# Blocks two and three of a Mamba-2 scan with an ELU layer behind it: twelve of sixteen groups through the word products instead of eight

## The chip, the cores and the metric

One Trainium2 chip, one of its cores. The metric is the device time of one execution in microseconds (us). The kernel before was run three times: 350.15 us in the median, 349.95 to 351.11. One further execution was profiled.

A core has engines that run beside each other, each taking its own instructions strictly in the order in which they were written: TensorE (PE in the profile, PEld for its weight loads), VectorE (DVE), ScalarE (ACT), GpSimd (POOL) and SyncE (SP, which issues most of the transfers). They meet only where one waits for another's semaphore.

## What is computed

A chunked state-space scan over four batches, eight heads and 768 tokens, and behind it a dense layer of width 2048 with ELU, all in float32 accuracy:

```python
cum = np.cumsum(log(a), axis=-1)                    # within a chunk
L   = np.exp(cum[..., :, None] - cum[..., None, :]) * causal
y   = ((C @ B^T) * L) @ x  +  (C @ state) * exp(cum)
state = exp(sum(log a)) * state + (B * exp(cum[-1] - cum))^T @ x

h = y @ w_in                      # [3072, 256] @ [256, 2048]
g = where(h > 0, h, exp(min(h, 0)) - 1)
out = g @ w_out                   # [3072, 2048] @ [2048, 256]
```

The weights arrive as 64-bit numbers and are turned into float32 on the chip.

## The kernel before, in words

**Blocks and groups.** The tokens are twelve blocks of 256, numbered 0 to 11; blocks go in pairs. The hidden width 2048 is sixteen groups `m` of 128, and eight pieces `i` of 256 (two groups each). `w_in` and `w_out` come as eight pieces each. Piece 0 to 7 is `w_in`, piece 8 + j is the part of `w_out` that `l2(n, j)` multiplies.

**Two ways for the first layer.** `l1(n, i)` (matmuls at L667) multiplies one block by one piece of `w_in` in plain float32: four products of 128x256, each of which is two passes in the trace, so eight records. Its ELU is `elu()`: a Relu and an Exp on ACT (L680, L687) and one subtraction with maximum on DVE (L689). `l1_words(n, m)` (L787) multiplies a pair of blocks (512 tokens) by one group, with numbers that were split into words: three passes, high word by high word and low by low into one PSUM tile `high`, the sum of words by the sum of words into another, `both`, two records each. Its end is longer: ACT scales `both` into e (L793), DVE combines it with `high` (L796), ACT takes Relu and Exp (L802, L803, in `begin_end`), DVE takes the maximum (L810, in `end_words`). **The order matters:** inside `l1_words` the L793 of this group is written first, then the L810 of the group before, then the L796 of this group; `begin_end` follows. For even groups `end_words` also subtracts one half of g from the other on POOL (L845).

**Words.** `words_of_w(i)` makes the high word of a piece of `w_in` on ACT (L736) and the sum of words on DVE (L737); `low_of_w(i)` the low word with two subtractions on POOL (L845). `words_of_y(n)` makes y1 on ACT (L755, L757; partly on DVE, L759) and y0 on DVE (L762); `both_of_y(n)` y_both with two operations on DVE (L772). y1 and y0 have one buffer each, so the words of the next pair can only be written when the last `l1_words` of this pair has read them.

**Second layer.** Blocks 0 and 1 go through `l2(n, j)` (L829). From block 2 on pairs go through `second(n)`, a seven-product scheme on sums and differences of quarters of g and of `w_out` (L904), whose quarters `quarters(n, i)` picks from g; those of pieces that went through `l1` lie otherwise than those that went through `l1_words`, and need a subtraction on DVE (`sum_t1`, L858).

**Making a piece of a weight.** `w_take(i, eng)` takes the absolute value on ACT (L196), the low part on the named engine (DVE at L209 or ACT at L205) and the sign on DVE (L223); `w_give(i)` clips (L231) and joins with the sign (L238) on DVE and adds the low part on POOL (L248, `w_sum`).

**The scan.** `spread_cum(n)` loads the running sums of a block, spread over the partitions, into a tile L (two buffers). `decay_of(n, h)` turns one head of it into exp(L - cum) with two small ACT instructions (L521, 128x64 each, the subtraction as the bias `ncum`), and after every fourth head two POOL instructions mask it (L526). `scores(n)` (L541), `sums(n)` (L571), `weigh(n, q)` (DVE, L550), `states(n)` (DVE L588 and POOL L593, which makes Sx), `across(n)` (L616) and `inside(n)` (L634, then copies into yT on ACT, L651) do the rest.

**PSUM.** Seven tiles of one bank are shared by everything but the sums of the second layer. An `l1` holds one until its L689 has run, an `l1_words` two until its L810; `scores` takes four.

**The order around the change** is written out by hand. A first loop, `for s, (n, i)`, has twelve `l1`: in its steps 0 to 7 it runs `decay_of(2, s)`, in step 7 `scores(2)` and `sums(2)`, in step 9 half of the decays of block 3, and in every odd step up to 11 one piece. A second loop, `for j in range(2 * DIRECT)`, runs `l2(0, j)` and one `l1` in each of eight steps (block 2 in the first four, block 3 in the others), pieces 11 to 15 of the weights in steps 0, 2, 3, 4 and 5, the scan of block 3, the decays of blocks 4 and 5 and the words of y. A third loop, `for j in range(8, 16)`, runs `l1_words(2, 8)` to `l1_words(2, 15)`, `l2(1, ...)` and the scan of blocks 4 and 5. Then a loop over pairs from block 4 on has sixteen `l1_words` each, with the products of `second` in between.

Of the kernel before, what the change touches and what calls it, by code (L numbers as in the profile page):

```python
# [20 lines left out]
CW = 256  # L21
WORD = 2.0 ** 12
NEAR = 1.0 + 2.0 ** -13
DIRECT = 4


def high_word_as_f32(word):
# [5 lines left out]
def kernel(  # L33
# [118 lines left out]
                w_load(piece)  # L152


    w_order = [(i + DIRECT) % (DF // CW) for i in range(DF // CW)]
    w_in = [None] * (DF // CW)
    for i in w_order:
        w_in[i] = conv.tile([P, KC, CW], F32, tag="w_in", name="w_in", bufs=DF // CW + 1)
# [306 lines left out]
    def turn_part(n, part):  # L465
        if part < 2:
            turn_square(n, 1 - part)
        elif part == 2:
            mask_heads(n)
        else:  # L470
            turn_exp(n)
# [41 lines left out]
    def decay(n, q):  # L513

        decay_of(n, 2 * q)
        decay_of(n, 2 * q + 1)

    def decay_of(n, h):
        L, row = st[n]["L"], rows_of(n).start + NG * h
        for u in range(2):  # L520
            nc.scalar.activation(  # L521
                L[:, h, u], L[:, h, u], ACT.Exp, bias=ncum[:, u, row:row + 1])
        if h % 4 == 3:
            for v in range(2):
                part = L[Q * v:Q * v + Q, h - 3:h + 1]
                nc.gpsimd.affine_select(  # L526
                    out=part, in_=part, pattern=[[0, 4], [0, 2], [1, Q]],
                    compare_op=ALU.is_ge, fill=0.0, base=0, channel_multiplier=-1)

# [218 lines left out]
    def words_of_y(n):  # L750

        y = yT[n // 2].rearrange("p k b u i -> p k (b u i)")
        y1 = conv.tile([P, KC, 2 * BLK], F32R, tag="y1", name="y1", bufs=1)
        y0 = conv.tile([P, KC, 2 * BLK], F32R, tag="y0", name="y0", bufs=1)
        nc.scalar.activation(y1[:, 1], y[:, 1], ACT.Copy, scale=NEAR / WORD)  # L755
        if n == 4:
            nc.scalar.activation(y1[:, 0], y[:, 0], ACT.Copy, scale=NEAR / WORD)  # L757
        else:
            nc.vector.tensor_scalar(  # L759
                out=y1[:, 0], in0=y[:, 0], scalar1=NEAR / WORD, scalar2=None, op0=ALU.mult)  # L760
        for k in range(KC):
            nc.vector.scalar_tensor_tensor(  # L762
                out=y0[:, k], in0=y1[:, k].bitcast(F32), scalar=WORD, in1=y[:, k],
                op0=ALU.mult, op1=ALU.subtract)
        y_words[n] = y1, y0
# [11 lines left out]
    def l1_words(n, m, between=None):  # L777

        cols = slice(m % 2 * P, (m % 2 + 1) * P)
        w, w0 = k_words[m // 2]  # L780
        w1, both_w, w0 = w[:, 0, :, cols], w[:, 1, :, cols], w0[:, :, cols]
        y1, y0, both_y = y_words[n]
        high, both = psum([P, 2 * BLK], "ps_h"), psum([P, 2 * BLK], "ps_w")
        passes = [(high, w1, y1), (high, w0, y0), (both, both_w, both_y)]
        for ps, lhs, rhs in passes if n > 2 and m == 0 else passes[2:] + passes[:2]:
            for k in range(KC):
                nc.tensor.matmul(  # L787
                    out=ps, lhsT=lhs[:, k], rhs=rhs[:, k], start=k == 0 and lhs is not w0,
                    stop=k == KC - 1 and lhs is not w1)
        if between:  # L790
            words_of_y(between)
        e = ffn.tile([P, 2 * BLK], F32, tag="e", name="e", bufs=2)
        nc.scalar.activation(e, both, ACT.Copy, scale=WORD)  # L793
        if late:
            end_words()
        nc.vector.scalar_tensor_tensor(  # L796
            out=high, in0=high, scalar=WORD - 1.0, in1=e, op0=ALU.mult, op1=ALU.add)
        late.append((n, m, high, e))
# [8 lines left out]
    def end_words():  # L807
        n, m, h, e = late.pop(0)
        g_of[n, m] = ffn.tile([P, 2, BLK], F32, tag=f"g{m % 2}", name="g", bufs=12)
        nc.vector.scalar_tensor_tensor(  # L810
            out=g_of[n, m].rearrange("p b i -> p (b i)"), in0=e, scalar=1.0, in1=h,
            op0=ALU.subtract, op1=ALU.max)
        if m % 2 == 0 and (n, m) != (2, 14):
            sub(g_of[n, m][:, 1], g_of[n, m][:, 1], g_of[n, m][:, 0])

    def row_of(n):
# [39 lines left out]
    def sum_t1(n, i, eng=nc.gpsimd):  # L856
        b11, b21, b12, b22 = quarters(n, i)
        eng.tensor_tensor(out=b12, in0=b12, in1=b11, op=ALU.subtract)  # L858
# [107 lines left out]
    def w_take(i, low):  # L966

        w_abs(i)
        w_low(i, low)
        w_sign(i)  # L970
# [117 lines left out]
    w_load(10)  # L1088
    write_flat(2)

    todo = 5
    for s, (n, i) in enumerate((
            (1, 0), (1, 1), (1, 2), (0, 4), (1, 3), (0, 5), (1, 4), (0, 6), (1, 5), (0, 7),
            (1, 6), (1, 7))):
        l1(n, i, parts=2 if s < 2 else 1)
        if s < 8:
            decay_of(2, s)
        if s == 7:
            st[0] = kept
            scores(2)  # L1100
            sums(2, 0, pool=p_o, tag="o", parts=(None, last))
            weigh(2, 0)
            weigh(2, 1)
        if s % 2 == 1 and todo < 11:
            w_take(todo, nc.vector)
            w_give(todo)
            w_load(todo + 6)
            todo += 1
        if s in (1, 3):
            load_bc(3, us=(s // 2,))  # L1110
        if s == 9:
            write_flat(0)
        if s == 4:
            scaled(2, nc.gpsimd)
        if s == 5:
            turn(2)
            turn_exp(2)
        if s == 4:
            load_x(3)
            spread_exp(3)  # L1120
        if s == 8:
            weigh(2, 2)
            weigh(2, 3)
            states(0, last)
            st.pop(0)
            states(2)
        if s == 9:
            decay(3, 0)
            decay(3, 1)
        if s == 10:  # L1130
            spread_cum(4)
            inside(across(2), 2)
        if len(lag) > 1:
            elu()
# [35 lines left out]
        for r in range(i, i + count):  # L1170
            sub(s_out[1][:, r], a_out[0][:, r], a_out[2][:, r])

    for j in range(2 * DIRECT):
        n, i = 2 + j // DIRECT, j % DIRECT
        if j < 7:
            l2(0, j)
        piece = todo < len(pieces) and j != 1
        if j == 0:
            elu()
        if piece:  # L1180
            w_take(todo, nc.vector)
        l1(n, i)
        if j == 7:
            l2(0, j)
        if j == 0:
            scaled(3, nc.gpsimd)
            turn(3)
            elu()
            turn_exp(3)
        if piece:  # L1190
            w_give(todo)
            todo += 1
        while lag:
            elu()
        if j == 0:
            decay(3, 2)
            decay(3, 3)
        if j == 1:
            scores(3)
            sums(3)  # L1200
            for q in range(4):
                weigh(3, q)
        if j == 2:
            states(3)
        if j == 3:
            inside(across(3), 3)
        if j == 4:
            words_of_y(2)
        if j == 4:
            words_of_w(4)  # L1210
        if j == 5:
            low_of_w(4)
        if j == 5:
            both_of_y(2)
        scan_ahead(j)
        if j == 3:
            s_out[:] = weight_sums()
        if j == 6:
            differences(0, 4)
        if j == 7:  # L1220
            words_of_w(5)
    for j in range(8, 16):
        i = j - 8
        l1_words(2, j)
        if i == 7:
            words_of_y(4)
        for p in ((), (6,), (), (7,), (0,), (1,), (2,), ())[i]:
            words_of_w(p)
        for p in ((5,), (), (6,), (7,), (0,), (), (), ())[i]:
            low_of_w(p)  # L1230
        if i == 7:
            l2(1, 6)
            l2(1, 7)
        begin_end()
        if i == 0:
# [6 lines left out]
        if i == 2:  # L1242
# [9 lines left out]
            for to in (6, 7):  # L1252
                load_b(to)
                spread_cum(to)
        if i == 3:
            l2(1, 3)
        if i == 4:
            y = across(4, 5)
            l2(1, 4, half=0)
            inside(y, 4, 5, ts=(0,))  # L1260
            l2(1, 4, half=1)
            inside(y, 4, 5, ts=(1,))
        if i == 5:
            l2(1, 5)
        if i in (0, 1, 3, 4):
            sum_t1(2, (0, 1, 3, 4).index(i), nc.vector)
        if i in (4, 6):
            turn_part(6, i // 2 - 2)
        if i in (2, 5):
            differences(4 if i == 2 else 6, 2)  # L1270
        if i < 6:
            sum_weights(nc.gpsimd, a_out, s_out, i)
    both_of_y(4)
    end_words()
    words_of_w(3)
    decay(6, 0)
    for p in (3, 1, 2):
        low_of_w(p)
    sum_t2(2, 0)
    sub(g_of[2, 14][:, 1], g_of[2, 14][:, 1], g_of[2, 14][:, 0])  # L1280
    left = (step for i in (6, 7) for step in weight_steps(nc.vector, a_out, s_out, i))

    def stage_scan(n, k):
# [101 lines left out]
```

## Time and profile before

| what | value |
|---|---|
| median of three runs | 350.15 us (349.95 to 351.11) |
| the profiled execution | 350.85 us, of which 349.1 us is its span |
| granted clock of TensorE | 1.00 over the whole span |
| PE busy | 339.9 us, 97% of the span |
| DVE, ACT, POOL busy | 259.0, 234.7, 216.8 us |
| stretch 27.5 to 50.2 us | first loop, PE busy throughout |
| stretch 50.2 to 84.3 us | second loop; PE idle for 1.02 us at 81.5 |
| stretch 84.3 to 115.7 us | `l1_words` of blocks 2 and 3 |
| 115.7 us to the end | pairs from block 4 on |

All times in the text are counted from the start of the span. The chain of work that ended last is PE for 87% of it. In a timeline a row gives start, length, engine, line, operation, output and inputs, shape, number of instructions merged, and in brackets the idle time before it and what ended that. Rows of several merged instructions give the length from the first start to the last end.

### The profile page before, as it was taken

How to read it: one execution, taken by the hardware profiler on the slowest of the kernel's cores; microseconds unless marked ns; L12 is line 12 of the kernel's file. 1: busy time of each engine (PE TensorE's matmuls, PEld its weight loads, DVE VectorE, ACT ScalarE, POOL GpSimd, SP SyncE). 2: the span in 40 equal slices, each digit the busy share in tenths (PEclk: the TensorE clock that was granted, in tenths of full speed). 3: DMA queues.
4: the chain of work that ended last, by engine and by line, in shares of the span. 5: the costliest groups of instructions: out<-in, count | busy, mean ns of one | idle time of the engine just before them, and what ended most of it. 6: DMA issues, size and time to landing. Idle time of an engine off the chain costs nothing.

```text
span 349.1 us, 9873 instructions
## 1 busy us (share of the span) xinstructions
PE 339.9 (97%) x3878; PEld 297.5 (85%) x3878; DVE 259.0 (74%) x515; ACT 234.7 (67%) x537; POOL 216.8 (62%) x338
## 2 busy tenths in 40 slices
PE   7889999998999999999999999999999999999996
PEld 4669888887777889988999988989988999999996
DVE  4898988879997889875878775888675756665232
ACT  5689989597748889657699447699557466565000
POOL 5554554566999599984196764196854174455760
PEclk9999999999999999999999999999999999999999
DMA  8878988470261331070431070320000100001002
GB/s 145 220 220 180 303 175 252 95 132 31 66 126 23 91 62 32 8 151 15 106 62 32 8 160 4 99 40 2 2 0 5 62 0 3 0 0 56 9 0 62
DMA packets 72727, 26.49 MB, mean 76 GB/s; under 512 B 57768, under 2 KB 67560, under 8 KB 72680
## 3 DMA queue, kind: packets, MB, share of 16 engines
q1 hardware_dynamic: 70360, 25.60, 31.4%
q8 instruction: 30, 0.49, 0.6%
q10 hardware_dynamic: 2320, 0.26, 0.5%
q14 instruction: 17, 0.14, 0.1%
HBM read 22.51 MB, written 3.34 MB: 74 GB/s over the span
## 4 chain that ended last, share of the span: by engine, by line
PE 87%; DVE 3%; DMA 3%; SPq 3%; ACT 1%; issue 1%; POOL 1%; DVEq 0%; POOLq 0%; ACTq 0%
PE ps_o L904 36%; PE ps_h L787 18%; PE ps_h L667 11%; PE ps_w L787 9%; PE ps_o L829 6%; PE ps_y L634 3%; DMA w<-in_moe_w_in_dram 2%; PE ps_g L541 2%; PE ps_y L616 2%; PE ps_st L571 1%; DMA bc<-in_C_dram 1%; DVE y_both L772 1%; SPq L116 1%; SPq L178 1%; PE ps_o L890 1%
## 5 line engine op out<-in xcount | busy, mean ns | idle before, releaser
L904 PEld LDWEIGHTS ps_o<-w_out,g 128*128 128x128 f32 x640 | 78.5, 191 | 3.5
L904 PE MATMUL ps_o<-w_out,g 128*128 128x128 f32 x640 | 80.1, 275 | 0.0
L802 ACT ACTIVATE e<-ps_h 128x512 f32<-128x512 f32 x72 | 43.0, 598 | 50.5 <-DVE ps_h L796 50.5
L810 DVE SCALAR_TENSOR_TENSOR g<-e,ps_h 128x512 f32<-128x512 f32 x72 | 49.3, 685 | 31.1 <-ACT e L803 30.8
L845 POOL TENSOR_TENSOR g<-g 128x256 f32<-128x256 f32 x36 | 26.5, 737 | 57.3 <-DVE g L810 57.2
L796 DVE SCALAR_TENSOR_TENSOR ps_h<-ps_h,e 128x512 f32<-128x512 f32 x72 | 50.1, 695 | 13.1 <-ACT e L793 10.0
L793 ACT ACTIVATE e<-ps_w 128x512 f32<-128x512 f32 x72 | 42.3, 587 | 15.0 <-PE ps_w L787 14.9
L787 PE MATMUL ps_w<-y_both,w_words 128*128 128x512 f32 x144 | 51.5, 437 | 0.1
L667 PE MATMUL ps_h<-yT,w_in 128*128 128x256 f32 (+1 forms) x208 | 45.2, 368 | 2.5 <-POOL w_in L248 1.6
L803 ACT ACTIVATE e<-e 128x512 f32<-128x512 f32 x72 | 45.5, 632 | 2.3
L787 PE MATMUL ps_h<-y,w_words 128*128 128x512 f32 x144 | 45.6, 398 | 0.0
L787 PE MATMUL ps_h<-y,w 128*128 128x512 f32 x144 | 45.0, 392 | 0.2 <-POOL w L845 0.2
L667 PEld LDWEIGHTS ps_h<-yT,w_in 128*128 128x128 f32 x208 | 36.3, 190 | 8.4 <-POOL w_in L248 3.6
L521 ACT ACTIVATE L<-L,ncum 128x64 f32<-128x64 f32 x160 | 42.2, 336 | 0.2
L904 PE MATMUL ps_o<-w_sum,g 128*128 128x128 f32 x304 | 38.6, 276 | 0.0
L904 PEld LDWEIGHTS ps_o<-w_sum,g 128*128 128x128 f32 x304 | 37.0, 192 | 1.3
L526 POOL TENSOR_SCALAR_AFFINE_SELECT L<-L 64x512 f32<-64x512 f32 x40 | 29.2, 731 | 9.6 <-ACT L L521 7.5
L787 PEld LDWEIGHTS ps_h<-y,w 128*128 128x128 f32 x144 | 27.0, 188 | 7.1 <-POOL w L845 0.7
L787 PEld LDWEIGHTS ps_h<-y,w_words 128*128 128x128 f32 x144 | 26.7, 188 | 6.2 <-issue 0.5
L829 PE MATMUL ps_o<-w_out,g 128*128 128x256 f32 x128 | 30.9, 384 | 1.0 <-POOL w_out L248 1.0
L845 POOL TENSOR_TENSOR g<-t,g 128x256 f32<-128x256 f32 x40 | 28.1, 734 | 5.8 <-PE ps_o L904 5.7
L845 POOL TENSOR_TENSOR g<-g,t 128x256 f32<-128x256 f32 x40 | 28.7, 747 | 0.2
(133 smaller groups left out, 535.9 us busy)
## 6 DMA issues: line engine op xcount, KB each, us to landing
L<-flat SPq DMA_DIRECT2D x20, 256.0 KB
w<-in_moe_w_out_dram SPq DMA_DIRECT2D x8, 512.0 KB
w<-in_moe_w_in_dram SPq DMA_DIRECT2D x7, 512.0 KB
xr<-in_x_dram SPq DMA_DIRECT2D x24, 128.0 KB
out_dram<-c_sum SPq DMA_DIRECT2D x9, 256.0 KB
bc<-in_B_dram SPq DMA_DIRECT2D x24, 64.0 KB
bc<-in_C_dram SPq DMA_DIRECT2D x22, 64.0 KB
ec<-flat_exp SPq DMA_DIRECT2D x10, 128.0 KB
```

Source lines behind the costliest of these rows:

```text
L521: nc.scalar.activation(L[:, h, u], L[:, h, u], ACT.Exp, bias=ncum[:, u, row:row + 1])
L526: nc.gpsimd.affine_select(out=part, in_=part, pattern=[[0, 4], [0, 2], [1, Q]], compare_op=ALU.is_ge, fill=0.0, base=0, channel_multiplier=-1)
L667: nc.tensor.matmul(out=ps[:, j, toks], lhsT=w_in[i][:, k, j * P:(j + 1) * P], rhs=yT[n // 2][:, k, n % 2].rearrange("p u i -> p (u i)")[:, ...
L787: nc.tensor.matmul(out=ps, lhsT=lhs[:, k], rhs=rhs[:, k], start=k == 0 and lhs is not w0, stop=k == KC - 1 and lhs is not w1)
L793: nc.scalar.activation(e, both, ACT.Copy, scale=WORD)
L796: nc.vector.scalar_tensor_tensor(out=high, in0=high, scalar=WORD - 1.0, in1=e, op0=ALU.mult, op1=ALU.add)
L802: nc.scalar.activation(e, high, ACT.Relu, scale=-1.0)
L803: nc.scalar.activation(e, e, ACT.Exp, scale=-1.0)
L810: nc.vector.scalar_tensor_tensor(out=g_of[n, m].rearrange("p b i -> p (b i)"), in0=e, scalar=1.0, in1=h, op0=ALU.subtract, op1=ALU.max)
L829: nc.tensor.matmul(out=o_of[n][:, ts], lhsT=g_of[n, j][:, m % 2, ts * P:(ts + 1) * P], rhs=w_out[:, m], start=(m == 0 and ts == 0), stop=( ...
L845: nc.gpsimd.tensor_tensor(out=out, in0=in0, in1=in1, op=ALU.subtract)
L904: nc.tensor.matmul(out=ps[:, ts], lhsT=b[:, ts * P:(ts + 1) * P], rhs=a[:, i], start=(i == chunk[0] and ts == 0), stop=(i == chunk[-1]), s ...
```

## The change

`DIRECT` goes from 4 to 2: of the groups of blocks 2 and 3, only 0 to 3 go through `l1` (pieces 0 and 1), and 4 to 15 through `l1_words`, in the order 8 to 15, 4 to 7. The `l2(0, j)` stay eight steps, with an `l1` only in steps 0, 1, 4 and 5. `l2(1, ...)` is spread over the longer loop, the last one behind the twelfth group. The decays of blocks 2 and 3 become wide: POOL adds `ncum` to half a block (`from_token`, 128x512), ACT takes one Exp of it (`wide_exp`, 128x512), POOL masks it, each a step of the first loop after the other. `w_take` of pieces 5 to 15 has its low part on ACT. Pieces 14 and 15 are both made in step 4 of the second loop, ahead of `words_of_y(2)`, whose y1 is now made on ACT alone. `words_of_y(4)` moves into the last `l1_words(2, 7)`, ahead of its L793.

```diff
-DIRECT = 4
+DIRECT = 2
...
+    def from_token(n, half, eng=nc.gpsimd):
+        part = st[n]["L"][:, 4 * half:4 * half + 4]
+        first_row = rows_of(n).start + 4 * NG * half
+        eng.tensor_tensor(
+            out=part, in0=part,
+            in1=ncum[:, :, first_row:first_row + 4 * NG:NG].rearrange(
+                "p u h -> p h u").unsqueeze(3).to_broadcast([P, 4, 2, Q]), op=ALU.add)
+    def wide_exp(n, half):
+        part = st[n]["L"][:, 4 * half:4 * half + 4]
+        nc.scalar.activation(part, part, ACT.Exp)
...
-        if n == 4:
+        if n < 6:
             nc.scalar.activation(y1[:, 0], y[:, 0], ACT.Copy, scale=NEAR / WORD)
...
-        for ps, lhs, rhs in passes if n > 2 and m == 0 else passes[2:] + passes[:2]:
+        for ps, lhs, rhs in passes if m == (8 if n == 2 else 0) else passes[2:] + passes[:2]:
...
+    def step(s):
+        for n, at in ((2, -1), (3, 7)):
+            for half in range(2):
+                if s == at + 2 * half + 2:
+                    mask(n, half)
+                if s == at + 2 * half:
+                    from_token(n, half)
+                if s == at + 2 * half + 1:
+                    wide_exp(n, half)
+    step(-1)
...
         l1(n, i, parts=2 if s < 2 else 1)
-        if s < 8:
-            decay_of(2, s)
+        step(s)
...
-            w_take(todo, nc.vector)
+            w_take(todo, nc.scalar)
...
-        if s == 9:
-            decay(3, 0)
-            decay(3, 1)
...
-    for j in range(2 * DIRECT):
-        n, i = 2 + j // DIRECT, j % DIRECT
+    direct = {0: (2, 0), 1: (2, 1), 4: (3, 0), 5: (3, 1)}
+    for j in range(8):
...
-            w_take(todo, nc.vector)
-        l1(n, i)
+            w_take(todo, nc.scalar)
+        if j in direct:
+            l1(*direct[j])
...
-        if j == 0:
-            decay(3, 2)
-            decay(3, 3)
+        if j == 4:
+            w_take(todo, nc.scalar)
+            w_give(todo)
+            todo += 1
...
-    for j in range(8, 16):
-        i = j - 8
-        l1_words(2, j)
-        if i == 7:
-            words_of_y(4)
-        for p in ((), (6,), (), (7,), (0,), (1,), (2,), ())[i]:
+    order = [8, 9, 10, 11, 12, 13, 14, 15, 4, 5, 6, 7]
+    for i, m in enumerate(order):
+        l1_words(2, m, between=4 if i == 11 else None)
+        for p in {1: (6,), 3: (7,), 5: (2,), 7: (3,), 9: (0,), 11: (1,)}.get(i, ()):
             words_of_w(p)
-        for p in ((5,), (), (6,), (7,), (0,), (), (), ())[i]:
+        for p in {0: (5,), 2: (6,), 4: (7,), 6: (2,), 8: (3,), 10: (0,)}.get(i, ()):
             low_of_w(p)
-        if i == 7:
-            l2(1, 6)
+        if i == 11:
             l2(1, 7)
...
-        if i == 3:
+        if i == 4:
             l2(1, 3)
-        if i == 4:
+        if i == 6:
             y = across(4, 5)
...
-        if i == 5:
-            l2(1, 5)
-        if i in (0, 1, 3, 4):
-            sum_t1(2, (0, 1, 3, 4).index(i), nc.vector)
+        if i in (8, 10):
+            l2(1, i // 2 + 1)
+        if i < 2:
+            sum_t1(2, i, nc.vector)
...
-        if i < 6:
-            sum_weights(nc.gpsimd, a_out, s_out, i)
+        if i % 2 == 0:
+            sum_weights(nc.gpsimd, a_out, s_out, i // 2)
     both_of_y(4)
     end_words()
-    words_of_w(3)
     decay(6, 0)
-    for p in (3, 1, 2):
-        low_of_w(p)
+    low_of_w(1)
     sum_t2(2, 0)
```

More of the change, by code (lines that the diff above doesn't have):

```diff
@@ L152, in load_x @@
                 w_load(piece)
-    w_order = [(i + DIRECT) % (DF // CW) for i in range(DF // CW)]
+    w_order = [4, 5, 6, 7, 2, 3, 0, 1]
     w_in = [None] * (DF // CW)
@@ L516, in decay, with mask @@
         decay_of(n, 2 * q + 1)
+    def from_token(n, half, eng=nc.gpsimd):
[8 more added lines that the diff above has]
+        nc.scalar.activation(part, part, ACT.Exp)
+    def mask(n, half):
+        for v in range(2):
+            part = st[n]["L"][Q * v:Q * v + Q, 4 * half:4 * half + 4]
+            nc.gpsimd.affine_select(
+                out=part, in_=part, pattern=[[0, 4], [0, 2], [1, Q]],
+                compare_op=ALU.is_ge, fill=0.0, base=0, channel_multiplier=-1)
     def decay_of(n, h):
@@ L523, in decay_of @@
         if h % 4 == 3:
[L524 to L528, printed above, removed]
+            mask(n, h // 4)
     def scores(*ns):
@@ L812, in end_words @@
             op0=ALU.subtract, op1=ALU.max)
-        if m % 2 == 0 and (n, m) != (2, 14):
+        if m % 2 == 0:
             sub(g_of[n, m][:, 1], g_of[n, m][:, 1], g_of[n, m][:, 0])
@@ L1262 @@
             inside(y, 4, 5, ts=(1,))
-        if i == 5:
-            l2(1, 5)
-        if i in (0, 1, 3, 4):
-            sum_t1(2, (0, 1, 3, 4).index(i), nc.vector)
[L1267 to L1270, printed above, removed]
-        if i < 6:
-            sum_weights(nc.gpsimd, a_out, s_out, i)
+        if i in (8, 10):
+            l2(1, i // 2 + 1)
+        if i < 2:
+            sum_t1(2, i, nc.vector)
+        if i in (6, 9):
+            turn_part(6, i // 3 - 2)
+        if i in (3, 7):
+            differences(4 if i == 3 else 6, 2)
+        if i % 2 == 0:
+            sum_weights(nc.gpsimd, a_out, s_out, i // 2)
     both_of_y(4)
     end_words()
-    words_of_w(3)
     decay(6, 0)
-    for p in (3, 1, 2):
-        low_of_w(p)
+    low_of_w(1)
     sum_t2(2, 0)
-    sub(g_of[2, 14][:, 1], g_of[2, 14][:, 1], g_of[2, 14][:, 0])
     left = (step for i in (6, 7) for step in weight_steps(nc.vector, a_out, s_out, i))
```

## The prediction, made before the result was known

> **What bounds the kernel now.** I read the page's busy shares first, then the chain of work that ended last, the waits, and the timelines of single engines from 27 to 120 us. PE is busy for 97% and is 87% of the chain. From 27.5 us to the end PE's timeline has one idle stretch worth naming:
>
> ```profile
> 82.54 1.99 PE L829 MATMUL ps_o<-w_out,g 128*128 128x256 f32 x8 [1.02 <-POOL w_out L248]
> ```
>
> So every PE instruction that goes is time won, as long as nothing else takes its place. What could: in the stage of `l1_words(2, m)`, DVE and ACT pass each group back and forth. DVE's L796 rows of groups 8 to 15, and ACT and DVE between two of them:
>
> ```profile
> 88.47 0.69 DVE L796 SCALAR_TENSOR_TENSOR ps_h<-ps_h,e 128x512 f32<-128x512 f32 x1
> ...
> 91.34 0.69 DVE L796 SCALAR_TENSOR_TENSOR ps_h<-ps_h,e 128x512 f32<-128x512 f32 x1
> ...
> 93.37 0.68 DVE L810 SCALAR_TENSOR_TENSOR g<-e,ps_h 128x512 f32<-128x512 f32 x1
> 93.97 0.69 DVE L796 SCALAR_TENSOR_TENSOR ps_h<-ps_h,e 128x512 f32<-128x512 f32 x1
> ...
> 100.65 0.69 DVE L796 SCALAR_TENSOR_TENSOR ps_h<-ps_h,e 128x512 f32<-128x512 f32 x1
> ...
> 103.27 0.69 DVE L796 SCALAR_TENSOR_TENSOR ps_h<-ps_h,e 128x512 f32<-128x512 f32 x1
> ...
> 113.93 0.69 DVE L796 SCALAR_TENSOR_TENSOR ps_h<-ps_h,e 128x512 f32<-128x512 f32 x1
> ```
>
> ```profile
> 92.06 0.60 ACT L802 ACTIVATE e<-ps_h 128x512 f32<-128x512 f32 x1 [0.61 <-DVE ps_h L796]
> 92.70 0.63 ACT L803 ACTIVATE e<-e 128x512 f32<-128x512 f32 x1
> ```
>
> L796 of a group is written behind L810 of the group before, which needs that group's Exp, which needs its Relu, which needs its own L796. That is a **loop**: L796, L802, L803, L810, next L796. Group 9 to 10 takes 2.63 us (91.34 to 93.97), 11 to 12 takes 2.62. It can't go faster, whatever PE does. Between 10 and 11 DVE has the scan of blocks 4 and 5 (M, S_new) and the step is 6.68 us. I call the first L796 of the stage H: 88.47. From H to the end of y_both for block 4 (116.06 + 1.29 = 117.35), which releases PE at 117.40, are 28.9 us. PE in the same stage has 3.10 us for one `l1_words` and one `l2` (84.18, 87.31, 90.41 on its timeline): the two are nearly as fast as each other.
>
> **The change, part by part.** Base: the profiled execution, 350.85 us (0.70 above the median).
>
> *PE's work.* An `l1` is 1.73 us (16 records in 3.46); four go: -6.92. An `l1_words` is 3.10 - 1.73 = 1.37; four come: +5.48. Sum -1.44. `l2` and the scan stay. The wait of 1.02 goes if piece 15 comes early.
>
> *Wide decays.* Removed on ACT: 32 small Exps, 0.24 apart (8 in 2.00). Added: four of 128x512, 0.63 like L803. Added on POOL: four additions of 128x512, which no row shows. The same kind with 128x256 costs 0.74 (L845), the unsigned 128x512 of L248 1.27, twice the first 1.47: between 0.74 and 1.47. I take 1.3, by L248. The cover is the question: the wide Exp waits for POOL, and ACT's queue stands behind it. ACT is free at 28.73 (its L687 at 28.10), POOL at 29.99 (its L248 at 28.72), so the Exp starts at 30.7 to 31.5 and ACT has lost 2.0 to 2.7 us where it was dense (one idle stretch of 0.55 from 28.9 to 49). At step 7 there is hardly room for this:
>
> ```profile
> 41.94 0.69 DVE L689 SCALAR_TENSOR_TENSOR g<-e,ps_h 128x512 f32<-128x512 f32 x1 [0.23 <-ACT e L687]
> ```
>
> ```profile
> 42.25 0.69 PE L541 MATMUL ps_g<-ctm,bct 32*64 32x128 f32 x32
> 42.87 0.66 PE L571 MATMUL ps_st<-xr,sc 64*32 64x64 f32 x40
> ```
>
> `scores(2)` takes four of seven banks, `l1(1, 4)` and `l1(0, 6)` hold two, so `sums(2)` needs the bank that this L689 frees at 42.63, a quarter of a microsecond ahead. With ACT about 2 us late (2.5 lost and 0.6 for the second half; 14 small Exps, 3.4, gone; two wide ones, 1.1, and three low parts of pieces, 1.7, come; the 0.55 absorbed), PE waits 1.3 to 2.0 us here.
>
> *Low parts on ACT.* Eleven times 0.57 there, 0.33 to 0.8 less on DVE. DVE had 1.6 and 1.8 us idle in the second loop, so only ACT's side counts.
>
> *Second loop.* The last wide Exp of block 3 stands ahead of the copies of yT(2) on ACT, and behind five Sx, a mask (1.4) and an addition on POOL: copies at 53 instead of 49.85. From there ACT's queue (copies 1.65, four ELUs and two pieces at 1.15 each) brings g(2, 0) to 62.6 instead of 58.9; DVE's M, piece 12 and S_new follow, and the Sx that `across(3)` needs come at 69.5 instead of 67.6. PE, with two `l1` less, is there at 67: it waits about 2.3. From the copies of yT(3) at 70.3 on, ACT has 10.75 us in a row (copies 1.65, eight small Exps 1.95, piece 14, ELU, piece 15 at 1.15 each, y1 1.05, words 0.55, four Exps 0.95, ELU 1.15), then 5.4 to the first L793. That puts **H at 86.8**; without the lateness at the wide Exps, 83.3; with no wait on PE at all, 88.47 - 6.92 - 1.02 = 80.5. I take 85.0, between the first two.
>
> *Third loop.* From H: 2.87, 2.63, 6.68 as now (the same work stands there); groups 12, 13, 14 at 2.63, 7.9; group 15 behind the copies of yT(4), 4.6; groups 4, 5, 6 at 2.63, 7.9: L796 of group 6 at H + 32.6. Then Relu and Exp 1.3, y1 1.04, y0 1.29, L810 and L796 1.2, words of piece 1 0.8, y_both 1.29: **H + 39.5**. Now it is 28.9: four more turns of the loop are 10.5; 0.9 us in which it waited for PE go; y_both, now straight behind y0, comes 1.0 later behind L810, L796 and a piece's words. PE's cover for this is one `l2` (1.73) and the high pass (0.92) behind group 7, where it was two `l2`. Fewer `sum_t1` (two of 0.84 on DVE) lie in holes where DVE waits for the Exp, and bring nothing. POOL has more here (three subtractions of g at 0.74, two pieces' low words at 1.4) but ends before the loop does.
>
> *Sum.* y_both at 85.0 + 39.5 = 124.5 instead of 117.35: +7.15. Behind it PE is dense to the end in the rows of before, so nothing is won back: 358.0 for the profiled execution, **357.3 us** against the median of 350.15. With H at 80.5 it is +2.65, at 86.8 +8.95.
>
> *A rule of the Trainium skill that speaks against the change.* The row first: y_both of block 2 takes 2.58 us for two instructions while POOL works beside it, that of block 4 takes 1.29 while POOL is idle:
>
> ```profile
> 81.59 2.58 DVE L772 SCALAR_TENSOR_TENSOR y_both<-y,yT 128x512 fp32r<-128x512 f32 x2
> ...
> 116.06 1.29 DVE L772 SCALAR_TENSOR_TENSOR y_both<-y,yT 128x512 fp32r<-128x512 f32 x2
> ```
>
> The Trainium skill, "SBUF — State Buffer", section "Who interferes with whom", says that a VectorE instruction with two SBUF inputs and a GpSimd one that reads SBUF exclude each other, while ScalarE waits for nobody. By that rule, and the trace agrees, the decays' additions move from an engine that disturbs nobody to one that can hold DVE: by the estimate of four blocks of 1.3 us the sum would be 5 us more, and nothing more where DVE's second input lies in PSUM, as in L796 and L810.
>
> **The rivals.**
>
> *PE stays the bound (faster).* PE's own work is 12 x 1.37, 8 x 1.73 and 4.6 for the scan of blocks 4 and 5, 34.9 us or 2.9 for each group, which is more than the loop's 2.63; were the 6.68 and the copies swallowed by the three groups that PSUM lets PE run ahead, only PE's sum would count: -1.44 - 1.02 - 0.5 (at 117.40) gives 347.9, 347.2 by the median. It decides itself where L796 of group 6 comes 27 us behind an H of 80.5, or 23 behind one of 85.0, not 32.6. Against it: the 6.68 is DVE's own work, and the first loop's rows show a quarter of a microsecond of room.
>
> *The loop costs, nothing else does.* H at 80.5, all waits ahead of it hidden: +2.65, 352.8. For it: POOL's price at the low end; ACT's relief of 32 small Exps. Against it: ACT's 28.73 against POOL's 29.99 is written in the rows.
>
> *PE's clock.* PE would be idle for some 5 us in one piece between group 7 and block 4, since y1 must wait for the Exp of group 6. The granted clock is 1.00 in all windows and no row of before has such a wait. If it fell to a half for one step of 3.10 us afterwards, 3.1 more: 360.4. The Trainium skill, "TensorE: Matmul & The Clock Gate", section "HAM oscillation — how this bites in real kernels", has such a fall behind idle gaps over about 3.4 us; no run here shows it.
>
> *The change doesn't do what it says.* Out: in the changed kernel's order the four wide Exps, four additions and twelve groups are there, and no small Exp of blocks 2 and 3 is left.
>
> **How the numbers follow.** The loop and a late H: 0.60. Clock: 0.10. The loop alone, up to +4: 0.18. PE stays the bound: 0.08. The gains and the losses cancel to within 0.3%, about what a measurement can tell: 0.04. So slower 0.88, same 0.04, faster 0.08. The range leaves out the last two cases and a little above the clock: 352.0 to 361.0.
>
> **What would show each step.** First loop: ACT idle ahead of the first wide Exp, PE idle ahead of L571 near 43. Second: Sx of block 3 near 69. Third: L796 rows 2.6 apart through groups 12 to 6, PE idle ahead of the first y_both pass of block 4. Wrong if PE stands dense there, if the L796 rows come closer than 2.6, or if the additions on POOL take far less than 1.3.

## The result and the profile after

The changed kernel takes 366.83 us (six runs, 365.73 to 368.6) where the kernel before takes 350.56: 1.0459 times as long, 95% interval 1.043 to 1.0489. I had forecast 357.3 and a range of 352.0 to 361.0. The direction was right, the size was not: the loss is 16.3 us, not 7.15. The profiled execution of the changed kernel takes 367.05 us with a span of 365.0, so 15.9 us of span are to be found. (Lines of the changed kernel are 16 higher: L812 is before's L796, L826 its L810, L788 its L772, L845 its L829.)

The row of the granted clock on the page is all nines before. After, it dips in three slices:

```profile
PEclk9999999898999969999999999999999999999999
```

PE's timeline of the kernel before at the three places that the text compares (start, duration, instruction):

```profile
67.62 0.80 PE L616 MATMUL ps_y<-bct,Sx 32*64 32x64 f32 x32
...
84.18 0.82 PE L787 MATMUL ps_w<-y_both,w_words 128*128 128x512 f32 x2
...
117.74 1.95 PE L904 MATMUL ps_o<-w_out,g 128*128 128x128 f32 x16
```

PE's timeline of the changed kernel, from the products of Sx for block 3 to the first pass of block 4 that needs `y_both` (in brackets the idle time ahead of an instruction and what ended it):

```profile
69.96 0.34 PE L632 MATMUL ps_y<-bct,Sx 32*64 32x64 f32 x8 [2.18 <-POOL Sx L609]
70.68 0.46 PE L632 MATMUL ps_y<-bct,Sx 32*64 32x64 f32 x24 [0.39 <-POOL Sx L609]
71.07 1.19 PE L650 MATMUL ps_y<-M,xr 64*32 64x64 f32 x64
72.19 3.14 PE L845 MATMUL ps_o<-w_out,g 128*128 128x256 f32 x8
...
83.61 0.82 PE L803 MATMUL ps_h<-y,w_words 128*128 128x512 f32 x2
...
126.22 0.73 PE L803 MATMUL ps_h<-y,w_words 128*128 128x512 f32 x2 [1.56 <-ACT y L773]
...
130.64 0.80 PE L803 MATMUL ps_w<-y_both,w_words 128*128 128x512 f32 x1 [2.53 <-DVE y_both L788]
131.76 0.79 PE L803 MATMUL ps_w<-y_both,w_words 128*128 128x512 f32 x1 [0.33 <-DVE y_both L788]
132.36 3.62 PE L920 MATMUL ps_o<-w_out,g 128*128 128x128 f32 x16
```

Three numbers divide the 15.9. The first pass over words (83.61) starts 0.6 earlier than before (84.18), although the second loop has four `l1` less on PE (6.92 us) and the wait of 1.02 is gone. From there to the point at which PE goes on behind block 4's first both pass are 48.75 us (132.36), where it was 33.56 (84.18 to 117.74): **15.2 more**. What lies behind takes 1.3 more; at its start PE runs at half its clock: sixteen matmuls of L920 take 3.62 us at 132.36 and 1.95 before.

DVE's rows show how the third stage fills those 48.75:

```profile
80.67 2.84 DVE L778 SCALAR_TENSOR_TENSOR y<-y,yT 128x512 fp32r<-128x512 f32 x2 [0.19 <-ACT y L773]
...
90.14 0.69 DVE L812 SCALAR_TENSOR_TENSOR ps_h<-ps_h,e 128x512 f32<-128x512 f32 x1
...
102.52 0.69 DVE L812 SCALAR_TENSOR_TENSOR ps_h<-ps_h,e 128x512 f32<-128x512 f32 x1
...
105.15 0.69 DVE L812 SCALAR_TENSOR_TENSOR ps_h<-ps_h,e 128x512 f32<-128x512 f32 x1
...
107.77 0.69 DVE L812 SCALAR_TENSOR_TENSOR ps_h<-ps_h,e 128x512 f32<-128x512 f32 x1
...
129.37 2.34 DVE L788 SCALAR_TENSOR_TENSOR y_both<-y,yT 128x512 fp32r<-128x512 f32 x2
```

The first L812, which the prediction calls H, is at 90.14. Of the eleven steps from one L812 to the next six are 2.63, as forecast; the others are longer, where DVE or ACT have the scan or the words of y in between. `y_both` ends at 131.71. H to that end: 41.6 us, forecast 39.5, before 28.9.

### The profile page after: what moved, and what is told of

Read it like the earlier page. It is cut to its first block, busy times and chain, and to the rows that moved or that the text cites. A ratio compares the mean times of both kernels' runs of the same rounds, so it can differ in the third digit from the quotient of the medians.

```text
span 365.0 us, 9841 instructions
## 1 busy us (share of the span) xinstructions
PE 347.4 (95%) x3870; PEld 301.2 (83%) x3870; DVE 255.3 (70%) x505; ACT 239.7 (66%) x525; POOL 223.6 (61%) x344
## 4 chain that ended last, share of the span: by engine, by line
PE 71%; DVE 8%; ACT 6%; DMA 5%; issue 3%; POOL 3%; SPq 3%; DVEq 0%; POOLq 0%; ACTq 0%
PE ps_o L920 35%; PE ps_h L803 17%; PE ps_w L803 9%; PE ps_o L845 3%; DMA w<-in_moe_w_out_dram 2%; PE ps_h L683 2%; PE ps_y L650 2%; DMA w<-in_moe_w_in_dram 2%; DVE ps_h L812 2%; PE ps_g L557 1%; ACT e L818 1%; DVE y_both L788 1%; ACT e L819 1%; PE ps_y L632 1%; POOL w_in L248 1%
## 5 line engine op out<-in xcount | busy, mean ns | idle before, releaser
L920 PEld LDWEIGHTS ps_o<-w_out,g 128*128 128x128 f32 x640 | 80.2, 195 | 3.5
L920 PE MATMUL ps_o<-w_out,g 128*128 128x128 f32 x640 | 81.8, 279 | 0.0
L826 DVE SCALAR_TENSOR_TENSOR g<-e,ps_h 128x512 f32<-128x512 f32 x76 | 52.0, 685 | 34.7 <-ACT e L819 34.4
L812 DVE SCALAR_TENSOR_TENSOR ps_h<-ps_h,e 128x512 f32<-128x512 f32 x76 | 52.8, 695 | 16.1 <-ACT e L809 11.8
L803 PE MATMUL ps_w<-y_both,w_words 128*128 128x512 f32 x152 | 55.7, 445 | 3.5 <-DVE y_both L788 3.4
L809 ACT ACTIVATE e<-ps_w 128x512 f32<-128x512 f32 x76 | 44.6, 587 | 18.8 <-PE ps_w L803 18.7
L819 ACT ACTIVATE e<-e 128x512 f32<-128x512 f32 x76 | 48.0, 632 | 2.5
L803 PE MATMUL ps_h<-y,w 128*128 128x512 f32 x152 | 48.1, 394 | 1.5 <-POOL w L861 1.2
L683 PE MATMUL ps_h<-yT,w_in 128*128 128x256 f32 (+1 forms) x176 | 37.8, 365 | 3.0 <-POOL w_in L248 1.9
L920 PE MATMUL ps_o<-w_sum,g 128*128 128x128 f32 x304 | 38.7, 276 | 0.0
L920 PEld LDWEIGHTS ps_o<-w_sum,g 128*128 128x128 f32 x304 | 37.0, 191 | 1.3
L683 PEld LDWEIGHTS ps_h<-yT,w_in 128*128 128x128 f32 x176 | 30.1, 190 | 8.2 <-POOL w_in L248 3.0
L541 ACT ACTIVATE L<-L,ncum 128x64 f32<-128x64 f32 x128 | 33.6, 337 | 0.0
L845 PE MATMUL ps_o<-w_out,g 128*128 128x256 f32 x128 | 33.4, 407 | 0.0
L803 PEld LDWEIGHTS ps_w<-y_both,w_words 128*128 128x128 f32 x152 | 24.9, 196 | 6.3 <-DVE y_both L788 4.5
```

The costliest lines, as they stand in the source:

```text
L541: nc.scalar.activation(L[:, h, u], L[:, h, u], ACT.Exp, bias=ncum[:, u, row:row + 1])
L683: nc.tensor.matmul(out=ps[:, j, toks], lhsT=w_in[i][:, k, j * P:(j + 1) * P], rhs=yT[n // 2][:, k, n % 2].rearrange("p u i -> p (u i)")[:, ...
L803: nc.tensor.matmul(out=ps, lhsT=lhs[:, k], rhs=rhs[:, k], start=k == 0 and lhs is not w0, stop=k == KC - 1 and lhs is not w1)
L812: nc.vector.scalar_tensor_tensor(out=high, in0=high, scalar=WORD - 1.0, in1=e, op0=ALU.mult, op1=ALU.add)
L819: nc.scalar.activation(e, e, ACT.Exp, scale=-1.0)
L826: nc.vector.scalar_tensor_tensor(out=g_of[n, m].rearrange("p b i -> p (b i)"), in0=e, scalar=1.0, in1=h, op0=ALU.subtract, op1=ALU.max)
```

## The experiments

Theory 1, with which I began: the wide Exps wait for POOL, ACT gets late, H with it, and the loop does the rest. Its rival, theory 2: ACT has too much work. The first four kernels undo one part of the change or do one part alone. Ratios are to the kernel before, run on the same chip beside each.

**Narrow decays in the changed kernel** (a1_narrow):

```
-    step(-1)
-        step(s)
+        if s < 8:
+            decay_of(2, s)
...
+        if s == 9:
+            decay(3, 0)
+            decay(3, 1)
...
+        if j == 0:
+            decay(3, 2)
+            decay(3, 3)
```

> The changed kernel with the decays of blocks 2 and 3 as they were: 32 small Exps with the token's bias at their old places, no addition on POOL; all else changed. Theory 1 (the wide Exps wait for POOL's additions, make ACT late, and PE's waits at 43 to 53 and at 70 us and the falls of its clock follow from that): PE's 4.8 us of waits ahead of the third loop go, the clock stays at 1.00 up to 85 us, the first L812 comes near 83 instead of 90.1, and the whole at 358 to 362 us. Theory 2 (ACT simply has too much work since the low parts of eleven pieces went to it): with 7.7 us of small Exps back on ACT it is no faster than 366.8, within 2 us.

Measured 367.69, ratio 1.0487 (1.0466 to 1.0507). H is at 91.2. The time is the one that theory 2 gave, not theory 1's 358 to 362: the waits at 43 to 53 are down to 1.3 us in all, but PE now waits 3.84 at 69.68 for Sx of block 3, and its clock falls there all the same. What the wide decays cost in the first loop is hidden by a later wait; theory 1 as the root is out.

**Low parts on DVE again** (a2_low_dve): `w_take(todo, nc.vector)` in both loops.

> The changed kernel with the low parts of pieces 5 to 15 on DVE again, all else changed. Theory 1: the low parts were filler on ACT, which waits for POOL and PE anyway: 364 to 369 us, H (the first L812) at 89 to 91. Theory 2 (ACT's load): eleven times 0.57 us less there, H three to five us earlier, 361 to 364 us.

Measured 367.71, ratio 1.0491 (1.0456 to 1.0526), H at 89.9, where theory 2 had 361 to 364 us: no gain from taking the work off ACT, so theory 2 is out as well. (This kernel puts the work on DVE, which is busy too; d1 below takes work off ACT and puts it nowhere.)

**The twelve groups alone** (a3_groups_alone): both edits above, and no second piece at j == 4. y1 on ACT alone and the high pass first in group 8 stay as in the change.

> The kernel before with only the twelve groups over words: narrow decays, low parts on DVE, piece 15 at its own turn. If the loop of 2.63 us a group sets the third stage: H at 80 to 83, from there 40 to 42 us to y_both of block 4, PE idle for some 4 us ahead of block 4, its clock halved once there (3 us): 357 to 362 us. If the loop is harmless and all the loss lies in the first two loops: 347 to 351 us.

Measured 366.69, ratio 1.0456 (1.0418 to 1.0493): the groups alone cost as much as the whole change, more than I expected of them (357 to 362), and H is at 90.84, not at 80 to 83. PE's timeline of this kernel shows no wait in the first loop, and then:

```profile
68.14 1.14 PE L632 MATMUL ps_y<-bct,Sx 32*64 32x64 f32 x32 [3.62 <-POOL Sx L609]
...
84.55 3.55 PE L845 MATMUL ps_o<-w_out,g 128*128 128x256 f32 x8 [3.23 <-POOL w_out L248]
```

The two waits are 6.85 us, and the four `l1` that went were 6.92. PE comes early to the scan's Sx and to the last piece of w_out, and waits for both. This led to theory 3: **the second loop is as long as the scan of block 3 and the pieces make it, and PE's saving there was never time.**

**The wide decays alone** in the kernel before (a4_wide_alone: the functions `from_token`, `wide_exp`, `mask` and `step` in place of the small Exps of blocks 2 and 3).

> The kernel before with only the wide decays: addition on POOL, Exp on ACT, mask on POOL, a step apart; eight groups over words, low parts on DVE. Theory 1: PE waits 1 to 2.5 us between 43 and 53 and about 2 us at 70, perhaps a fall of the clock of 1.7 us: 352 to 357 us. If the wide decays are harmless by themselves and only hurt beside the rest: 349 to 351 us.

Measured 355.47, ratio 1.0152 (1.0097 to 1.0208). Alone they do cost what theory 1 said, though the wait of 2 us near 70 that I expected with it isn't there. PE waits 0.82 at 43.15, and 1.89 ahead of the first `l1` of block 2, which then runs at half its clock (3.62 for what takes 1.89):

```profile
53.79 3.62 PE L687 MATMUL ps_h<-yT,w_in 128*128 128x256 f32 x8 [1.89 <-ACT yT L671]
```

So 1.5% of the wide decays and 4.6% of the groups make 4.6% together: the prices don't add up, as they wouldn't if both parts draw on the same slack.

**The saved products put back** (h1_l1_kept), the test of theory 3:

```
+    unread = {2: (2, 2), 3: (2, 3), 6: (3, 2), 7: (3, 3)}
...
+        if j in unread:
+            l1(*unread[j])
+            lag.pop()
```

> The changed kernel with the products of the four l1 that it saves put back on PE at their old places in the second loop (6.92 us of PE work whose sums nobody reads; no ELU, nothing on ACT or DVE); all else changed. Theory 3 (the second loop's length is that of the scan, the pieces and ACT's and DVE's queues, so PE's saving there was never time): within 2 us of the changed kernel, 365 to 369 us, PE's wait for Sx of block 3 gone or below 1 us and no fall of the clock near 71. Rival (PE's work counts, the loss is elsewhere): 6 to 7 us slower, 372 to 375 us.

Measured 365.46, ratio 1.0443 (1.0428 to 1.0458). PE does 6.92 us more and the kernel is no slower. Its timeline at the place where it waited:

```profile
68.76 1.89 PE L683 MATMUL ps_h<-yT,w_in 128*128 128x256 f32 x8
70.58 0.49 PE L632 MATMUL ps_y<-bct,Sx 32*64 32x64 f32 x32
70.99 0.90 PE L650 MATMUL ps_y<-M,xr 64*32 64x64 f32 x64
71.82 1.99 PE L845 MATMUL ps_o<-w_out,g 128*128 128x256 f32 x8
```

The products of Sx end at 71.07 here and at 71.14 in the changed kernel; the wait became work, and the clock stays up there. (It falls at 44.5 instead, and behind 126 for longer; the mean granted clock of both profiled executions is 0.981, so no gain from the clock hides a price.) The first pass over words starts 1.9 us later than in the changed kernel, at 85.55, and yet H comes 1.2 earlier, at 88.93. Theory 3 stands: taking the four `l1` out of the second loop brought nothing.

**What sets the way from the yT copies to H?** (d1_no_exps): `decay(...)` in `scan_ahead` replaced by `pass`, so that the kernel leaves out the decays of blocks 4 and 5 with their masks.

> The changed kernel without the decays of blocks 4 and 5 in the second loop: 32 small Exps (7.8 us of ACT) and eight masks (5.9 us of POOL) are left out, so the output of these blocks is not the reference's. Theory 3 with ACT's queue as the limit from the yT copies of block 3 to H: H at 83 to 87 instead of 90.1, 359 to 363 us. If DVE, POOL's pieces or PE's halved clock are the limit there: H at 88.5 to 90, 364.5 to 367 us.

Measured 366.67, ratio 1.0477 (1.0461 to 1.0494), H at 89.48. ACT's Exps are not the limit: with them gone, ACT stands ahead of the ELU of `l1(3, 0)`, behind which y1 is queued, and waits for PE, which runs at half its clock; later it waits for the first both pass (ACT's timeline of this kernel):

```profile
76.52 0.60 ACT L696 ACTIVATE e<-ps_h 128x512 f32<-128x512 f32 x1 [2.31 <-PE ps_h L683]
...
87.28 0.60 ACT L809 ACTIVATE e<-ps_w 128x512 f32<-128x512 f32 x1 [2.74 <-PE ps_w L803]
```

That both pass itself waits 1.65 for DVE's `y_both`, and DVE is busy without a break from its y0 at 80.08 to H. PE's clock isn't the limit either: h1, with the clock at 1.00 there, has H at 88.93.

**The words of block 2 ahead of the last pieces** (c1_words_first): `words_of_y(2)` behind `inside(across(3), 3)`, `both_of_y(2)` at j == 4.

> The changed kernel with y1 and y0 of block 2 straight behind the yT copies of block 3, and y_both one step of the second loop earlier, ahead of the last two pieces of w_out (which the change had put first). Theory 3 (ACT's and DVE's queue order behind the yT copies sets H): y_both at 78 to 82 instead of 85.6, H at 85 to 88, 362 to 365 us. Rival (PE, with piece 15 now later again, sets H): no gain, 366 to 369 us.

Measured 366.74, ratio 1.0451 (1.0413 to 1.0489): H at 88.68, `y_both` at 81.59 instead of 85.57, and 0.67 us of PE's wait for piece 15 are back at 82.85. The time doesn't move, which is what the rival said, though H did come 1.5 earlier. I read this as two or three queues with one deadline, where moving one uncovers another. On the way to H, ACT's L809 stayed where it was (88.05 in the changed kernel), and DVE's L812 followed sooner:

```profile
87.94 0.60 ACT L809 ACTIVATE e<-ps_w 128x512 f32<-128x512 f32 x1 [0.38 <-PE ps_w L803]
```

```profile
88.68 0.69 DVE L812 SCALAR_TENSOR_TENSOR ps_h<-ps_h,e 128x512 f32<-128x512 f32 x1
```

**Each wide Exp and mask a step later** (b2_later).

```
-                if s == at + 2 * half + 2:
+                if s == at + 2 * half + 3:
-                if s == at + 2 * half + 1:
+                if s == at + 2 * half + 2:
```

> The changed kernel with each wide Exp and its mask one step later than now, so that POOL's addition is done before ACT comes to it. PE's waits at 43 to 53 us (2.25 us) should go. Theory 3 (the stretch from the yT copies of block 3 to H is 17.5 to 21 us of ACT's and DVE's queues in every kernel, and Sx of block 3 comes no earlier than 68): H at 88.5 to 90, 363.5 to 366.5 us. Theory 1 (the wait for POOL is the root): H near 85, 360 to 362.5 us.

Measured 365.83, ratio 1.0425 (1.0379 to 1.0471). The wait of 1.16 at 53 is gone, of the two near 43 one of 0.71 is left; that of 2.18 for Sx stays (now at 68.70), and H is at 88.68. Theory 3 had it right.

**The clock.** Fillers (products of a zero column into banks that are open anyway) in PE's idle stretches, first b1_fill:

```
+    def nothing(out, count, m=0):
+        for _ in range(count):
+            nc.tensor.matmul(
+                out=out, lhsT=zero.to_broadcast([P, P]), rhs=w_out[:, m],
+                start=False, stop=False, skip_group_check=True)
```

> The changed kernel with products of a zero column on PE in its idle stretches: twelve of 128x256 ahead of the Sx products of block 3, eight around the first group over words, seven ahead of the last l2 of block 1 and twelve between the low and the both pass of block 4's first group. They add nothing to the sums. If the falls of the clock follow PE's idle stretches: granted clock 1.00 in all windows from 60 to 140 us, the 2.7 us lost behind 130 us come back, and up to 2 us of the late H: 361 to 364.5 us. If the falls don't follow idleness, or the fillers delay PE as much: 366 to 369 us.

Measured 368.61, ratio 1.0503 (1.0464 to 1.0543): the clock of the profiled execution is at 1.00 throughout, but I had counted a filler as 0.22 us and it takes 0.44, so they delayed the copies of yT(3) by 2.3 us. Inconclusive on the price, clear on the cause: with PE's idle stretches filled the clock doesn't fall. Half as many, b4_fill_half:

> As the first kernel with fillers, with half as many of them (5, then 3 around the first group over words, 3 and 6), since one product of 128x256 took 0.44 us and not 0.22, and the fillers themselves made the copies of yT and block 4's both pass about 2.3 us late. Clock at 1.00 throughout, or one short fall. If the falls cost what the halved rows show (1.2 near 72, up to 1.9 behind 130): 363 to 365.5 us. If something else hides them: 366 to 367.5 us.

Measured 364.41, ratio 1.0415 (1.0396 to 1.0435), clock 1.00 throughout the profiled execution. Two stretches of the changed kernel and the same two of this one (width, PE busy, granted clock, DMA's share, GB/s):

```profile
70.00:80.00 10.00, 9.62 (x127) 0.83 0.70 132
130.00:140.00 10.00, 9.03 (x43) 0.70 0.49 100
```

```profile
70.00:80.00 10.00, 9.59 (x133) 1.00 0.85 131
130.00:140.00 10.00, 9.36 (x61) 1.00 0.48 83
```

By the ratios the falls cost 1.5 us (the two intervals just meet), by the two profiled executions 2.8, of which 1.0 lie ahead of the point behind block 4's first both pass (131.34 instead of 132.36) and 1.8 behind it. The 1.8 are not settled: f1 below has the clock at 1.00 behind that point and takes 232.7 us from there to the end of the span, as the changed kernel does (232.6; before 231.4).

**The loop opened** (b3_ahead): the Relu, Exp and L826 of a group go behind the next group's L809 and L812.

```
-        if late:
+        if late and n > 2:
             end_words()
...
-        begin_end()
+        if i == 11:
+            both_of_y(4)
+        if i:
+            begin_end(0)
+            end_words()
```

> The changed kernel with the loop of the third stage opened: a group's Relu, Exp and L826 stand behind the next group's L809 and L812 (a third buffer for e, in the place of tmp), y1, y0 and y_both of block 4 straight behind the last group's L812, and both last l2 of block 1 behind the last group as PE's cover. If the loop of 2.63 us a group sets the third stage: PE becomes its bound (34.9 us), block 4's first pass near 121 to 123 instead of 126.2, no idle stretch and no fall of the clock there: 355 to 360 us. If DVE, ACT or POOL hold the same pace without the loop: 363 to 367 us.

Measured 364.04, ratio 1.0366 (1.0319 to 1.0414): 2.8 us less than the changed kernel by the medians, 3.3 by the ratios, 4.5 by the profiled executions. DVE's rows are no longer 2.63 apart:

```profile
101.81 0.69 DVE L812 SCALAR_TENSOR_TENSOR ps_h<-ps_h,e 128x512 f32<-128x512 f32 x1
...
103.75 0.69 DVE L812 SCALAR_TENSOR_TENSOR ps_h<-ps_h,e 128x512 f32<-128x512 f32 x1
105.18 0.70 DVE L812 SCALAR_TENSOR_TENSOR ps_h<-ps_h,e 128x512 f32<-128x512 f32 x1 [0.16 <-PE ps_h L803]
...
126.65 1.28 DVE L788 SCALAR_TENSOR_TENSOR y_both<-y,yT 128x512 fp32r<-128x512 f32 x2
```

The time lies between my two cases, nearer to the one in which other queues hold the pace: block 4's first pass is at 124.78, not at 121 to 123, and 83.98 to 128.32 are 44.3 us, against 48.75 with the loop and before's 33.6. The loop cost some 4 us. The rest stays when it is opened.

**All three remedies** (f1_open_later: b3, b2 and c1 together).

> The changed kernel with the three remedies together: the loop of the third stage opened, each wide Exp and mask a step later, and the words of block 2 straight behind the yT copies of block 3. Theory 3 (PE's saving in the second loop is no time, its 5.48 us more in the third stage are): H at 86 to 88.5, PE dense in the third stage for 36 to 37 us, 358 to 362 us, still slower than before by 8 or more. Rival (the waits were the whole loss, and twelve groups without them are as good as eight): 347 to 353 us.

Measured 361.04, ratio 1.0311 (1.029 to 1.0333). Still 11 us over before. PE's timeline:

```profile
83.49 0.82 PE L803 MATMUL ps_h<-y,w_words 128*128 128x512 f32 x2
...
126.18 1.10 PE L803 MATMUL ps_w<-y_both,w_words 128*128 128x512 f32 x2 [0.65 <-DVE y_both L788]
127.11 1.95 PE L922 MATMUL ps_o<-w_out,g 128*128 128x128 f32 x16
```

The stage starts 0.7 earlier than before and takes 43.6 us instead of 33.6: PE is busy for 6.7 more (39.68 against 32.95; four groups are 5.5 by my count) and idle for 3.3 more (seven waits of 0.4 to 0.65, for low words from POOL, y0 and `y_both`, where before had two of 0.2). Another 1.3 lie behind the stage. This is theory 3's case (358 to 362): twelve groups lose even without the waits I could remove.

**The wide decays alone, a step later** (f2_wide_later: a4 with b2's edit).

> The kernel before with only the wide decays, each Exp and mask a step later than the change has them. If the loss of 4.9 us was the Exp's wait for POOL's addition: PE's waits of 0.8 and 1.9 us at 43 and 53 and the fall of the clock at 54 go, 349.3 to 351.5 us. If it was POOL's and ACT's work itself: 353 to 356 us.

Measured 351.45, ratio 1.0040 (1.0026 to 1.0053) where a4 had 1.0152: 1.1 of the 1.5% were the Exp's wait for the addition and the fall of the clock behind it. What is left is 1.6 us, at the upper end of what I expected: the wide decays don't gain. PE still waits 0.56 at 42.57, where before it didn't.

**The last piece alone** (e1_piece_alone), and with f2's decays (g1_piece_wide):

```
-        for ps, lhs, rhs in passes if n > 2 and m == 0 else passes[2:] + passes[:2]:
+        for ps, lhs, rhs in passes if m == (8 if n == 2 else 0) else passes[2:] + passes[:2]:
...
+        if j == 4:
+            w_take(todo, nc.vector)
+            w_give(todo)
+            todo += 1
```

> The kernel before with only the last piece of w_out in the step of the piece before it, ahead of the words of block 2, and the first group over words with its high pass first. If the wait of 1.02 us at 82.54 simply goes: 349.0 to 349.9 us. If ACT and DVE make y1, y0 and y_both later by the piece's 1.2 to 1.5 us instead: 350.2 to 352 us.

Measured 349.34, ratio 0.9979 (0.9968 to 0.999): **faster than the kernel before**, by 0.7 us. The wait of 1.02 at 82.54 is gone and nothing took its place; PE's timeline:

```profile
80.63 1.89 PE L829 MATMUL ps_o<-w_out,g 128*128 128x256 f32 x8
82.17 0.80 PE L787 MATMUL ps_h<-y,w_words 128*128 128x512 f32 x2
```

> The kernel before with the last piece ahead of the words of block 2 (which alone gave 349.34) and the wide decays with the Exp a step later. If PE is the limit and both only move other engines' work: 348.8 to 349.8 us, no better than the piece alone. If ACT's 32 small Exps still cost something in the second loop: below 348.8 us. If the additions on POOL still cost PE waits: above 350 us.

Measured 350.80, ratio 1.0026 (1.0012 to 1.0039): with the wide decays the gain is lost again (PE waits 0.53 at 42 and 0.39 at 85).

## Why the prediction was wrong

The span grew by 15.9 us and I had forecast 7.15. Of the 8.75 between them 5.1 are H, 2.1 the way from H to the end of `y_both`, and 1.5 lie behind it, where I had counted nothing.

*PE's work, -1.44 and -1.02.* The saving was counted rightly, but in the second loop it is worth nothing: h1 puts 6.92 us of it back at no cost. In the profile before, PE was 97% busy, and I took that as proof that its saving was time, up to what H gave back. But Sx of block 3 came no earlier than 68 even in a3, where PE stood ready at 64.5, and before, PE itself came at 67.62: the scan was as long as PE's own work.

*First loop.* Right in size, only in part in place. Near 43 I had forecast 1.3 to 2.0 us and PE waits 1.09 (0.77 and 0.32); its rows name DVE's ctm and POOL's addition as what ended the waits, not the L689 that I had named. Another 1.16 follow behind the copies of yT(2), which came at 53.0 as forecast. A large addition on POOL took 1.24 and 1.37 us at first, where I took 1.3, and 1.06 and 1.11 later.

*Second loop up to Sx.* Right in size: the wait forecast at 2.3 was 2.18 and 0.39; the products of Sx end at 71.1. But I laid it to the lateness on ACT; a3 and a1 show it as large without wide decays.

***H at 85.0* is the step that failed.** It came at 90.14, in the changed kernel and between 88.68 and 91.8 in every kernel with twelve groups except f1 (87.68). Of the 5.1 us, 1.8 are my choice to stand between the walk along ACT's queue (86.8) and a case in which PE's saving counted (83.3); by h1 that saving doesn't count, and even the walk was too early. 1.5 are yT(3), whose copies came at 71.77, not 70.3, behind the second wait and at half PE's clock. ACT's queue itself I had walked rightly (the first L809 is 16.3 behind the yT copies, walked 16.15):

```profile
88.05 0.60 ACT L809 ACTIVATE e<-ps_w 128x512 f32<-128x512 f32 x1
```

The last 1.7 are DVE. I let L812 follow 0.35 behind the start of L809, and it came 2.1 behind, since DVE is busy without a break from 80.67 to H, its two y0 taking 2.84 beside POOL's addition and masks. c1 bears this out: it moves y1, y0 and `y_both` ahead, L809 stays at 87.94, and L812 follows at 88.68. The rival with H at 80.5 (2.65 us) has the same error, larger.

*The loop.* Right in kind and size: 2.63 a turn, four turns more, L812 of group 6 at H + 33.0 where I had 32.6, and opened it gives 2.8 to 4.5 us back. H to the end of `y_both` was 2.1 longer than forecast, half of it in `y_both` itself: 2.34 where b3, with POOL idle just then, has 1.28. I had taken 1.29. The Trainium skill, "SBUF — State Buffer", section "Who interferes with whom", which I weighed for the decays, states the cause that fits: a VectorE instruction with two SBUF inputs and GpSimd's reads exclude each other. The trace agrees (2.34 beside POOL's subtractions, 1.28 without), but at another place than the one where I priced it; no run takes POOL's work away there and leaves all else.

*PE's clock.* A rival at 0.10, with one fall at 3.1 us. There were three, and the one ahead of block 4's both pass came where I had put it. Together they cost 1.5 to 2.8 by b4. It should have been a part of the forecast, since I forecast the idle stretch itself.

*The part that was right for the change*, the last piece ahead, I named only as 1.02 of PE's wait. Alone it gives 0.7.

Open: why the wide decays without their wait still cost 0.4%; why the stretch behind block 4's first both pass is 1.3 us longer in f1 too, at full clock; what PE could gain in the second loop if the scan's Sx came earlier, which wasn't tried.

## What to carry to other kernels

A busy engine is the bound only if the other chains of that stage are clearly shorter: before work is taken off it, look at what it would wait for next, and put the work back as unread products to see whether it was ever time. Work that is moved out of a stage in which other chains set the pace, into one that is dense, saves nothing in the first and costs at least its own time in the second, and the prices of the parts of one change need not add up. A walk down one engine's queue has to be checked against the other engine that ends the step.

## What the hardware showed

Three falls of PE's clock to 0.50 in one kernel, at 71.15, 88.2 and 129.15 us, 17 and 41 us apart (5 and 12 times 3.4), lasting about 3.4, 3.4 and 6.8 us. In the 3.4 us ahead of them PE was busy for 0.84, 2.16 and 1.67 us, and no single idle stretch was over 2.6. The Trainium skill, "TensorE: Matmul & The Clock Gate", section "HAM oscillation — how this bites in real kernels", speaks of idle gaps over about 3.4 us; here shorter ones in a row were enough. The busy time of a stretch laid anywhere doesn't tell it alone: f2 has a stretch of 3.4 us with 2.10 busy, b3 one with 1.78, and their clocks stay at 1.00 there, while h1's fell behind one with 2.25. With PE's gaps filled (b1, b4) the clock stayed at 1.00.
